# Loading q and k of a fused attention kernel by half batches into rings, and writing the result over the gate's tile

## The chip, the core and the metric

The kernel runs on one core of a Trainium2 chip. The time is the device time of one execution, in microseconds (us), as the median of several executions. Beside that there is one profiled execution, whose trace gives the start and the length of every instruction on each engine: TensorE (PE in the profile), VectorE (DVE), ScalarE (ACT), GpSimd (POOL, which does next to nothing here) and SyncE (SP), which issues the DMA transfers.

## What is computed

Attention within chunks of 64 tokens, on 8 batches of 8 heads, 576 tokens and 64 values per head, in float32; its heads side by side are the input x of a channel mix with 512 columns in and 1024 inside. Cut to what matters:

```python
# _attn_ref: q, k, v of [8, 8, 576, 64], chunks of 64 tokens
scores = scale * np.matmul(q_c, k_c.transpose(0, 1, 2, 4, 3))
scores = scores - np.max(scores, axis=-1, keepdims=True)
attn = np.exp(scores)
attn = attn / (np.sum(attn, axis=-1, keepdims=True) + 1e-09)
out = np.matmul(attn, v_c)
# _moe_ref: x of [8, 576, 512]
x_prev = np.concatenate([np.zeros((B, 1, D)), x[:, :-1, :]], axis=1)
xk = mu_k * x + (1.0 - mu_k) * x_prev
xr = mu_r * x + (1.0 - mu_r) * x_prev
k = np.maximum(xk @ w_k, 0.0)
v = k * k @ w_v
r = 1.0 / (1.0 + np.exp(-(xr @ w_r)))
return r * v
```

## The kernel before

The 8 x 576 tokens are one row of 4608, cut into 18 groups of 256 tokens (two tiles of 128). Since 576 is no multiple of 256, groups 2, 4, 6, 11, 13 and 15 lie across two batches; all but group 2, which the start loads in another layout, are loaded by `load_blocks`. Products that need more than one pass are done with operands split into a high and a low part (`xkhi`, `xklo`, `xrhi`, `xrlo`).

Two programs, written as strings of words, set the order of every instruction on every engine: nothing is moved by a scheduler. `START` sets up the weights and does groups 0 and 1 and the attention of group 2. `GROUP` is one period; `group(g)` emits it for g = 2 to 17 (this text calls it period g). Period g does the channel mix of group g, the attention of group g + 1, and the loads for groups after it. A word names a task and the steps of it that are emitted there:

- `Sc` are the scores of group g + 1 (64 matmuls in line 988, the first thing on PE in each period), the maximum, the exp and the sums behind them; `Pq` turns the normed p (line 1044) and multiplies it with v into `xps` (line 1062), from which x comes.
- `K0` to `K3` are the product with w_k (line 613), the relu and the square; `R0`, `R1` that with w_r (line 666) and the sigmoid, whose result is the gate's tile `sg` (five of them in turn).
- `V0`, `V1` (`moe_v`, periods 2 and 3, g < `SPLIT` = 4) are the product with w_v as it is (line 697), and `B`, `C` prepare pieces of w_v in these two periods; from period 4 on `H`, `Z` and `W` (`moe_halves`, line 887) do it with fewer products and more sums. The last step of either multiplies with the gate into a tile `out` (line 711 or 932), which is stored.
- `Lq`, `Lk` load q and k of group g + 3 (line 201), `Lv` the two v tiles of group g + 2 (line 180). `Dq.0` and `Dq.1` turn q and k of group g + 2 on DVE, whole tiles of 128 x 1024 in place (line 969). `Mk`, `Mr`, `Md` mix x with its predecessor.

All loads and stores are issued on SP, in the order of the words. One load of q or k for a group is 16 transfers, each for 32 of the 128 partitions and one of four pairs of heads, of 8 blocks of 32 tokens; where the group lies across two batches (`segments`) each of them is issued twice, so that there are 32:

```python
for s, n in segments(g * G, G):
    b, t0 = divmod(g * G + s, S)
    for j in range(2):
        for dh in range(2):
            for hp in range(HP):
                nc.sync.dma_start(out=dst[pp : pp + 32, hp, s // 32 : (s + n) // 32, :], in_=...)
```

The tiles for q and k are two each (pool `ld`), so the load for group g + 3 takes the tile whose group g + 1 has just had its scores. Groups 3 and 4 (`bq3`, `bk3`, `bq4`, `bk4`) are loaded in `START`, where v of tiles 6 and 7 (`v6`, `v7`) is loaded too.

Of the kernel before, what the change touches and what calls it, by code (L numbers as in the profile page):

```python
# [7 lines left out]
F32 = mybir.dt.float32  # L8
# [8 lines left out]
P = 128  # L17
CH = 64
# [63 lines left out]
def tile_chunk_attention_channel_mix(  # L82
# [13 lines left out]
    B, H, S, D = q.shape  # L96
# [6 lines left out]
    NG = B * S // G  # L103
# [5 lines left out]
    ld = ctx.enter_context(tc.tile_pool(name="ld", bufs=2))  # L109
# [46 lines left out]

    def load_nat(g):
        for nm, src in (("q", q), ("k", k)):
            do.task = f"n{nm}{g}"

            def fn(_, nm=nm, src=src):
                dst = T[f"{nm}{g}"] = ld.tile([P, H, 2, D], F32, tag=nm, name=f"{nm}n_{g}")
# [26 lines left out]
    def load_blocks(g):  # L189
        for nm, src in (("q", q), ("k", k)):  # L190
            do.task = f"b{nm}{g}"

            def fn(_, nm=nm, src=src):
                dst = T[f"{nm}{g}"] = ld.tile([P, HP, G // 32, 32], F32, tag=nm, name=f"{nm}_{g}")
                for s, n in segments(g * G, G):
                    b, t0 = divmod(g * G + s, S)
                    for j in range(2):
                        for dh in range(2):
                            pp = j * 64 + dh * 32
                            for hp in range(HP):  # L200
                                nc.sync.dma_start(  # L201
                                    out=dst[pp : pp + 32, hp, s // 32 : (s + n) // 32, :],
                                    in_=src[
                                        b, j * HP + hp, t0 : t0 + n, dh * 32 : (dh + 1) * 32
# [153 lines left out]

    def att_qk(t):

        g, tl = divmod(t, 2)
        tb = slice(tl * (TT // 32), (tl + 1) * (TT // 32))
        do.task = f"D{t}"
        for nm in "qk":

            def f_move(_, nm=nm):
                x = T[f"{nm}{g}"][:, :, tb, :]
                nc.vector.transpose(out=x, in_=x)

            do(f_move, "D")  # L370
# [314 lines left out]
    def moe_v(g, tls):  # L685
# [118 lines left out]
    def moe_halves(g):  # L804
# [122 lines left out]
        def scale(t, c, src):  # L927
            def fn(_):
                if f"o{g}{t}" not in T:
                    T[f"o{g}{t}"] = mo.tile([P, DM], F32, tag="out", name=f"out_{g}_{t}")  # L930
# [346 lines left out]
```

## Time and profile before

| | |
|---|---|
| median of 3 executions | 610.05 us (609.01 to 610.32) |
| the profiled execution | 606.43 us |
| its span in the trace | 604.5 us |
| granted TensorE clock, mean | 0.994 |
| busy PE, DVE, ACT | 98%, 76%, 59% of the span |

The span runs from the first to the last instruction of the trace, and the execution's own time is 1.93 us longer. Busy shares are means over the whole span; the place where an engine bounds the time is found in the chain of waits, which follows the work that ended last back to what released it, and in the timeline of an engine, which lists its instructions in order with the idle time in front of each and who ended it. For SP a row is a run of DMA issues, from the first issue to the last.

### The profile page before, as it was taken

The page shows a single profiled execution, that of the slowest core. Times are in us where ns is not written, and L with a number is a line of the kernel's source. Part 1 is how long each engine was busy: PE and PEld are TensorE (multiplying, and loading weights), DVE is VectorE, ACT ScalarE, POOL GpSimd, SP SyncE. Part 2 cuts the span into 40 slices and gives each one's busy share as a digit, 9 for nine tenths or more (in the row PEclk, how much of TensorE's full clock was granted, in tenths as well). Part 3 has the DMA queues.
Part 4 walks back from the last instruction along what each step waited for, and adds up shares of the span by engine and source line. Part 5 has one row for each costly group of instructions (what it writes and reads, how often), then busy time and mean ns, then how long its engine had stood idle before and what let it go on. Part 6 is the DMA issues. An engine that isn't in the chain of part 4 may idle for free.

```text
span 604.5 us, 15523 instructions
## 1 busy us (share of the span) xinstructions
PE 590.9 (98%) x6497; PEld 556.3 (92%) x6497; DVE 458.8 (76%) x743; ACT 355.1 (59%) x530; POOL 0.7 (0%) x6
## 2 busy tenths in 40 slices
PE   8899999999999999999999999999999999999997
PEld 7779999989997999999999999999997999999997
DVE  2799887659788687878787878887887488876734
ACT  4898963625647383838383838383828174646461
POOL 0000000000000000000000000000000000000000
PEclk9999999999999999999999999999999899999999
DMA  9995323244124344343122441243323343010000
GB/s 283 232 315 133 89 51 76 36 96 102 30 34 96 72 96 101 61 97 68 54 35 41 103 103 31 34 101 68 79 35 86 62 107 71 36 37 36 1 36 36
DMA packets 187573, 49.28 MB, mean 82 GB/s; under 512 B 173160, under 2 KB 179312, under 8 KB 187504
## 3 DMA queue, kind: packets, MB, share of 16 engines
q1 hardware_dynamic: 187488, 48.29, 35.6%
q8 instruction: 51, 0.84, 0.6%
q14 instruction: 18, 0.15, 0.1%
q10 hardware_dynamic: 16, 0.00, 0.0%
HBM read 38.80 MB, written 9.44 MB: 80 GB/s over the span
## 4 chain that ended last, share of the span: by engine, by line
PE 79%; SPq 13%; DVE 3%; DMA 2%; issue 2%; ACT 1%; DVEq 0%
PE pk L613 29%; PE pr L666 14%; PE vx L887 11%; SPq L201 10%; PE vyz L887 8%; PE pv L697 6%; SPq L180 3%; PE xps L1062 2%; PE s L988 2%; PE pt L1044 1%; DMA v<-in_v 1%; PE trq L345 1%; PE trk L345 1%; DMA qn<-in_q 1%; PE mxk L557 1%
## 5 line engine op out<-in xcount | busy, mean ns | idle before, releaser
L613 PE MATMUL pk<-xkhi,wk 128*128 128x256 f32 x1152 | 210.1, 283 | 0.0
L613 PEld LDWEIGHTS pk<-xkhi,wk 128*128 128x128 f32 x1152 | 178.2, 188 | 1.2
L613 PE MATMUL pk<-xklo,wk 128*128 128x256 f32 x576 | 162.3, 282 | 0.0
L633 ACT ACTIVATE rr<-pk 128x512 f32<-128x512 f32 x56 | 33.2, 592 | 128.7 <-PE pk L613 128.7
L613 PEld LDWEIGHTS pk<-xklo,wk 128*128 128x128 f32 x576 | 108.6, 189 | 0.1
L666 PE MATMUL pr<-wr,xrhi 128*128 128x512 f32 x288 | 95.2, 412 | 0.0
L887 PE MATMUL vx<-b,ks 128*128 128x256 f32 x504 | 66.7, 282 | 0.0
L666 PEld LDWEIGHTS pr<-wr,xrhi 128*128 128x128 f32 x288 | 52.7, 192 | 11.0
L887 PEld LDWEIGHTS vx<-b,ks 128*128 128x128 f32 x504 | 62.8, 189 | 0.0
L666 PE MATMUL pr<-wr,xrlo 128*128 128x512 f32 x144 | 57.8, 401 | 0.0
L697 PE MATMUL pv<-b,kk 128*128 128x256 f32 x384 | 46.7, 282 | 0.0
L697 PEld LDWEIGHTS pv<-b,kk 128*128 128x128 f32 x384 | 46.1, 188 | 0.3
L887 PE MATMUL vyz<-b,kk 128*128 128x256 f32 x336 | 44.5, 282 | 0.0
L887 PEld LDWEIGHTS vyz<-b,kk 128*128 128x128 f32 x336 | 41.9, 189 | 0.0
L724 DVE TENSOR_TENSOR kk<-rr,kk 128x1024 fp32r<-128x1024 f32 x28 | 33.1, 1222 | 9.3 <-ACT kk L871 9.1
L724 DVE TENSOR_TENSOR xklo<-mk,xkhi 128x1024 fp32r<-128x1024 f32 x15 | 18.4, 1225 | 24.5 <-ACT xkhi L1134 24.5
L916 ACT ACTIVATE u<-vx 128x256 f32<-128x256 f32 x28 | 10.7, 384 | 44.0 <-PE vx L887 44.0
L640 ACT ACTIVATE rr<-rr 128x512 f32<-128x512 f32 x56 | 35.4, 632 | 1.8
L666 PEld LDWEIGHTS pr<-wr,xrlo 128*128 128x128 f32 x144 | 27.7, 192 | 6.6
L1017 DVE TENSOR_REDUCE z<-p 128x16 f32<-128x1024 f32 x15 | 18.3, 1220 | 18.3 <-ACT p L1013 18.3
L1124 DVE SCALAR_TENSOR_TENSOR mk<-d,mu,x 128x256 f32<-128x256 f32 (+3 forms) x80 | 27.7, 413 | 0.4
L1062 PEld LDWEIGHTS xps<-pT,v 64*64 64x64 f32 x960 | 17.5, 137 | 10.9 <-DMA v<-in_v 5.1
(138 smaller groups left out, 957.1 us busy)
## 6 DMA issues: line engine op xcount, KB each, us to landing
v<-in_v SPq DMA_DIRECT2D x144, 64.0 KB, 2.4
out<-out SPq DMA_DIRECT2D x36, 256.0 KB, 2.4
k<-in_k SPq DMA_DIRECT2D x160, 32.0 KB, 1.9
q<-in_q SPq DMA_DIRECT2D x160, 32.0 KB, 2.0
wk_st<-in_moe_w_k SPq DMA_DIRECT2D x4, 1024.0 KB, 11.2
wv_st<-in_moe_w_v SPq DMA_DIRECT2D x4, 1024.0 KB, 8.8
wr_st<-in_moe_w_r SPq DMA_DIRECT2D x2, 1024.0 KB, 7.6
q<-in_q SPq DMA_DIRECT2D x48, 24.0 KB, 1.8
```

Source lines behind the costliest of these rows:

```text
L180: nc.sync.dma_start(out=vt[j * CH : (j + 1) * CH, :, e, :], in_=v[b, j * HP : (j + 1) * HP, c * CH : (c + 1) * CH, :].rearrange("h t d -> ...
L201: nc.sync.dma_start(out=dst[pp : pp + 32, hp, s // 32 : (s + n) // 32, :], in_=src[b, j * HP + hp, t0 : t0 + n, dh * 32 : (dh + 1) * 32].r ...
L613: nc.tensor.matmul(pk[:, e, :], wk[a][:, cb, f * P : (f + 1) * P], xk[b][:, cb, :], start=(n == 0), stop=(n == 3 * NB - 1),)
L633: nc.scalar.activation(r, T[f"pk{g}{fp}"], AF.Relu)
L640: nc.scalar.activation(r, r, AF.Square)
L666: nc.tensor.matmul(pr, xr[a][:, cb, tl * TT : (tl + 1) * TT], wr[b][:, cb, :], start=(n == 0), stop=(n == 3 * NB - 1),)
L697: nc.tensor.matmul(T[f"pv{g}{tl}"][:, cols[c]], kk[a][:, f, tok[tl]], quarter(f // HF, c)[:, b, f % HF, :], start=(f == 0 and n == 0 and c ...
L724: nc.vector.tensor_tensor(to, x, y, ALU.subtract)
L887: nc.tensor.matmul(to, a[i][:, f, :], weight(w, j, f), start=first and f == 0 and n == 0, stop=f == HF - 1 and n == 2, skip_group_check=True,)
L1017: nc.vector.tensor_reduce(out=T[f"z{g}"], in_=p(), axis=AX.X, op=ALU.add)
L1062: nc.tensor.matmul(T[f"xps{g}"][halves[c], 2 * j + a, tl * TT + e * CH : tl * TT + (e + 1) * CH], T[f"v{2 * g + tl}"][halves[j], hp, e, :] ...
L1124: nc.vector.scalar_tensor_tensor(out=to[:, cb, s : s + w], in0=T[f"d{g}"][:, cb, s : s + w], scalar=mu[:, cb : cb + 1], in1=T[f"xg{g}"][:, ...
```

## The change

q and k get one tile each for the whole run, a ring of 18 blocks of 32 tokens (one batch of 576 tokens), in place of two tiles of 8 blocks. What is loaded at a time is a half batch m of 9 blocks, in 16 transfers for q and 16 for k; a half batch never lies across two batches. `START` loads the 12 blocks 24 to 35 in one go in place of groups 3 and 4 (32 transfers of 12 blocks; `bq4` and `bk4` are gone), and half batch m = 4 to 15 is loaded in the period that `load_period` gives, which is the first whose scores are the last readers of the slots: periods 2 to 7 and 9 to 14, none in period 8.

The turn of a group is cut in two: `De`, the blocks that lay there before this period, stands where `Dq.0` stood, for q and for k; `Dl`, the blocks that come with this period's load, stands late in the period, behind `B.3` in periods 2 and 3 and behind `W.11` from period 4 on. A turn whose blocks run over the ring's end is two instructions. There are late turns of 4, 3, 2, 1 blocks in periods 2 to 5 and of 6, 5, 4, 3, 2, 1 in periods 9 to 14. The score matmuls read their columns from the rings.

The result is no longer a tile of its own: the product with the gate is written over the gate's tile `sg`, and the store reads that.

```diff
@@ START
-hwv3.1:D bq4.0 S5.3:A V001.6 V001.7 P4.1:A S5.4:D K13.3:A S5.5:D P4.2 K11.1:A K13.4:D D7.1:D
+hwv3.1:D S5.3:A V001.6 V001.7 P4.1:A S5.4:D K13.3:A S5.5:D P4.2 K11.1:A K13.4:D D7.1:D
...
-V10.3 V11.2 V11.3 Mk5.0:D V10.4 Mk5.1:D Mr4.1:A V11.4 D7.0:D bk4.0 Mk4.2:A V10.5 v6.0 V10.6
+V10.3 V11.2 V11.3 Mk5.0:D V10.4 Mk5.1:D Mr4.1:A V11.4 D7.0:D Mk4.2:A V10.5 v6.0 V10.6
...
@@ GROUP
-Sc.0 K0.0 Lq Lk Sc.1 Sc.2 K0.12 Mr.0 Dq.0 Sc.3 K0.34 K1.0 K1.12 E.0 Mr.1 Sc.4567 Mr.2 K1.34 K2.0 K2.12 E.1 H.0 K2.34
-K3.0 Pq.0 K3.12 Dq.1 Z.0 Pq.1 K3.34 Z.1 H.1 H.3 Z.2 H.4 Z.3 H.2 H.5 Z.456
+Sc.0 K0.0 Lq Lk Sc.1 Sc.2 K0.12 Mr.0 De.01 Sc.3 K0.34 K1.0 K1.12 E.0 Mr.1 Sc.4567 Mr.2 K1.34 K2.0 K2.12 E.1 H.0 K2.34
+K3.0 Pq.0 K3.12 Z.0 Pq.1 K3.34 Z.1 H.1 H.3 Z.2 H.4 Z.3 H.2 H.5 Z.456
...
-V0 V1.0 W.0 W.1 W.2 W.5 W.6 W.7 Mk.1 C.0 C.2 C.4 W.8 B.2 Mk.2 B.3456 C.1 C.3 C.5 V1.12345678 W.9 W.10 W.12 W.11 W.3 W.4 W.13 W.14 W.15 W.16
+V0 V1.0 W.0 W.1 W.2 W.5 W.6 W.7 Mk.1 C.0 C.2 C.4 W.8 B.2 Mk.2 B.3 <Dl.01 B.456 C.1 C.3 C.5 V1.12345678 W.9 W.10 W.12 W.11 >Dl.01 W.3 W.4 W.13 W.14 W.15 W.16
...
-    ld = ctx.enter_context(tc.tile_pool(name="ld", bufs=2))
+    ld = ctx.enter_context(tc.tile_pool(name="ld", bufs=1))
...
+    NBLK = S // 32
+    HB = NBLK // 2
+    ring = {nm: ld.tile([P, HP, NBLK, 32], F32, name=f"{nm}_ring") for nm in "qk"}
+
+    def slots_of(first, many):
+
+        a = first % NBLK
+        n = min(many, NBLK - a)
+        return [(0, a, n)] + ([(n, 0, many - n)] if n < many else [])
...
-    def load_blocks(g):
+    def load_blocks(name, first, many):
+        b, s = divmod(first, NBLK)
+        assert s + many <= NBLK
...
-                dst = T[f"{nm}{g}"] = ld.tile([P, HP, G // 32, 32], F32, tag=nm, name=f"{nm}_{g}")
-                for s, n in segments(g * G, G):
-                    b, t0 = divmod(g * G + s, S)
+                for n0, a, n in slots_of(first, many):
+                    t0 = (s + n0) * 32
                     for j in range(2):
                         for dh in range(2):
                             pp = j * 64 + dh * 32
                             for hp in range(HP):
                                 nc.sync.dma_start(
-                                    out=dst[pp : pp + 32, hp, s // 32 : (s + n) // 32, :],
+                                    out=ring[nm][pp : pp + 32, hp, a : a + n, :],
...
+    def turn(nm, first, many):
+        for _, a, n in slots_of(first, many):
+            x = ring[nm][:, :, a : a + n, :]
+            nc.vector.transpose(out=x, in_=x)
...
-                o = mo.tile([P, DM], F32, tag="out", name=f"out_{g}_{tl}")
+                o = T[f"sg{g}{tl}"]
                 nc.vector.tensor_tensor(o, T[f"pv{g}{tl}"], T[f"sg{g}{tl}"], ALU.mult)
...
-                o = T[f"o{g}{t}"]
-                nc.vector.tensor_tensor(o[:, cols[c]], src(), T[f"sg{g}{t}"][:, cols[c]], ALU.mult)
+                o = T[f"sg{g}{t}"]
+                nc.vector.tensor_tensor(o[:, cols[c]], src(), o[:, cols[c]], ALU.mult)
...
     def group_scores(g):
-        do.task = f"D{g}q"
-        for nm in "qk":
-
-            def f_move(_, nm=nm):
-                nc.vector.transpose(out=T[f"{nm}{g}"], in_=T[f"{nm}{g}"])
-
-            do(f_move, "D")
+        b0, b1 = 8 * g, 8 * g + 8
+        m = (b1 - 1) // HB
+        late = max(b0, HB * m) if load_period(m) == g - 2 else b1
+        for part, (first, last) in enumerate(((b0, late), (late, b1))):
+            do.task = f"D{g}{'el'[part]}"
+            for nm in "qk":
+                if first < last:
+                    do(lambda _, nm=nm, first=first, last=last: turn(nm, first, last - first), "D")
+
+    def load_period(m):
+
+        return max(2, -(-(HB * m - 25) // 8))
...
-    load_blocks(3)
-    load_blocks(4)
+    load_blocks("3", 24, 12)
...
     def group(g):
-        if g + 3 < NG:
-            load_blocks(g + 3)
+        now = [m for m in range(4, 2 * B_) if load_period(m) == g]
+        for m in now:
+            load_blocks(f"m{m}", HB * m, HB)
...
         for word in GROUP.split():
+            if word[0] in "<>":
+                if (word[0] == "<") != (g < SPLIT):
+                    continue
+                word = word[1:]
```

SP, from the second half of the start to the loads of period 2, before. `in_q`, `in_k` and `in_v` are the arrays in memory, `q_...`, `k_...`, `v_...` the tiles; `32x4x32` is partitions x blocks x tokens of one transfer.

```order
L201 DMA q_1009<-in_q 32x8x32 x16
L180 DMA v_1032<-in_v 64x4x64 x4
L201 DMA q_1134<-in_q 32x4x32 x32
L180 DMA v_1221<-in_v 64x4x64 x4
L713 DMA out<-out_0_1233 128x512
L713 DMA out<-out_1_1268 128x512
L201 DMA k_1385<-in_k 32x4x32 x32
L180 DMA v_1427<-in_v 64x4x64 x4
L713 DMA out<-out_1_1473 128x512
L713 DMA out<-out_0_1477 128x512
L201 DMA q_1541<-in_q 32x8x32 x16
L201 DMA k_1558<-in_k 32x8x32 x16
```

The same place now:

```order
L218 DMA q_ring<-in_q 32x12x32 x16
L196 DMA v_1026<-in_v 64x4x64 x4
L196 DMA v_1182<-in_v 64x4x64 x4
L727 DMA out<-sg_0_625 128x512
L727 DMA out<-sg_1_628 128x512
L196 DMA v_1353<-in_v 64x4x64 x4
L218 DMA q_ring<-in_q 32x9x32 x2
L727 DMA out<-sg_1_906 128x512
L218 DMA q_ring<-in_q 32x9x32
L727 DMA out<-sg_0_884 128x512
L218 DMA q_ring<-in_q 32x9x32 x13
L218 DMA k_ring<-in_k 32x9x32 x16
```

The 32 + 32 transfers of 4 blocks are gone, three of the v loads follow each other with only stores between them, and period 2 loads 9 blocks where it loaded 8.

SP in period 3, before, where group 6 lies across two batches:

```order
L201 DMA q_1952<-in_q 32x6x32 x16
L201 DMA q_1952<-in_q 32x2x32 x16
L201 DMA k_1985<-in_k 32x6x32 x16
L201 DMA k_1985<-in_k 32x2x32 x16
L180 DMA v_2193<-in_v 64x4x64 x4
L180 DMA v_2198<-in_v 64x4x64 x4
L713 DMA out<-out_0_2290 128x512
L713 DMA out<-out_1_2359 128x512
```

and now:

```order
L218 DMA q_ring<-in_q 32x9x32 x16
L218 DMA k_ring<-in_k 32x9x32 x16
L196 DMA v_2081<-in_v 64x4x64 x4
L196 DMA v_2086<-in_v 64x4x64 x4
L727 DMA out<-sg_0_2091 128x512
L727 DMA out<-sg_1_2111 128x512
```

Each of q and k is 16 transfers of 9 blocks where it was 16 of 6 and 16 of 2.

DVE at the end of period 2 and the head of period 3, before. `bs` are the sums of pieces of w_v (`B`), `out` the result, `m` and `p` the maximum and the exponent of the next scores, `mr` the mixed x, `kk` the squares:

```order
L724 TENSOR_TENSOR bs_1771<-bs_1771 128x1024
L743 TENSOR_TENSOR bs_1772<-b_876 128x1024
L724 TENSOR_TENSOR bs_1771<-bs_1772,bs_1771 128x1024
L724 TENSOR_TENSOR bs_1772<-bs_1772,bs_1771 128x1024
L711 TENSOR_TENSOR out_1_1891<-pv_1_1835,sg_1_1769 128x512
L1004 TENSOR_REDUCE m_2018<-s_1894 128x16
L1010 TENSOR_TENSOR p_2020<-s_1894,m_2018 128x2x8x64
L1124 SCALAR_TENSOR_TENSOR mr_2027<-d_1774,mu_100,x_1753 128x256 x4
L969 STREAM_TRANSPOSE q_1541<-q_1541 128x1024
L649 TENSOR_TENSOR kk_3_2035<-relu_0_2022,kk_3_2034 128x512
```

and now:

```order
L738 TENSOR_TENSOR bs_1693<-bs_1693 128x1024
L379 STREAM_TRANSPOSE q_ring<-q_ring 128x4x128
L379 STREAM_TRANSPOSE k_ring<-k_ring 128x4x128
L757 TENSOR_TENSOR bs_1694<-b_871 128x1024
L738 TENSOR_TENSOR bs_1693<-bs_1694,bs_1693 128x1024
L738 TENSOR_TENSOR bs_1694<-bs_1694,bs_1693 128x1024
L725 TENSOR_TENSOR sg_1_1691<-pv_1_1756,sg_1_1691 128x512
L1024 TENSOR_REDUCE m_1906<-s_1816 128x16
L1030 TENSOR_TENSOR p_1908<-s_1816,m_1906 128x2x8x64
L1144 SCALAR_TENSOR_TENSOR mr_1915<-d_1696,mu_100,x_1675 128x256 x4
L379 STREAM_TRANSPOSE q_ring<-q_ring 128x4x160
L379 STREAM_TRANSPOSE k_ring<-k_ring 128x4x160
```

Two turns of 4 blocks stand between the sums of `B`, and at the head of period 3 q and k are turned together, 5 blocks (4 x 160 columns) each.

DVE at the end of period 9, before; `u` are the sums of `moe_halves`, `vx` and `vyz` its products:

```order
L923 TENSOR_TENSOR u_9_4837<-u_9_4837,vx_4822 128x256
L932 TENSOR_TENSOR out_1_4904<-u_9_4837,sg_1_4811 128x256
L923 TENSOR_TENSOR u_9_4836<-u_9_4836,vyz_4823 128x256
L932 TENSOR_TENSOR out_0_4907<-u_9_4836,sg_0_4793 128x256
L923 TENSOR_TENSOR u_9_4836<-u_9_4836,vyz_4823 128x256
L932 TENSOR_TENSOR out_1_4904<-u_9_4836,sg_1_4811 128x256
L932 TENSOR_TENSOR out_0_4907<-vx_4822,sg_0_4793 128x256
L1004 TENSOR_REDUCE m_5050<-s_4926 128x16
L1010 TENSOR_TENSOR p_5052<-s_4926,m_5050 128x2x8x64
```

and now:

```order
L937 TENSOR_TENSOR u_9_4643<-u_9_4643,vx_4628 128x256
L944 TENSOR_TENSOR sg_1_4617<-u_9_4643,sg_1_4617 128x256
L379 STREAM_TRANSPOSE q_ring<-q_ring 128x4x192
L379 STREAM_TRANSPOSE k_ring<-k_ring 128x4x192
L937 TENSOR_TENSOR u_9_4642<-u_9_4642,vyz_4629 128x256
L944 TENSOR_TENSOR sg_0_4599<-u_9_4642,sg_0_4599 128x256
L937 TENSOR_TENSOR u_9_4642<-u_9_4642,vyz_4629 128x256
L944 TENSOR_TENSOR sg_1_4617<-u_9_4642,sg_1_4617 128x256
L944 TENSOR_TENSOR sg_0_4599<-vx_4628,sg_0_4599 128x256
L1024 TENSOR_REDUCE m_4822<-s_4732 128x16
```

Two turns of 6 blocks stand in front of the last sums, and the product with the gate goes into `sg`.

## Rows read from the trace of the kernel before

**Rows 1.** The page: busy shares, and DMA issues (KB each, us to landing).
```profile
PE 590.9 (98%) x6497; PEld 556.3 (92%) x6497; DVE 458.8 (76%) x743; ACT 355.1 (59%) x530; POOL 0.7 (0%) x6
...
q<-in_q SPq DMA_DIRECT2D x160, 32.0 KB, 2.0
```

**Rows 2.** The chain of waits in order of time: start us, us, engine, line.
```profile
138.75 1.09 PE s L988 x64
...
170.57 1.09 PE s L988 x64
...
203.22 1.09 PE s L988 x64
...
233.61 1.09 PE s L988 x64
...
311.84 2.99 PE pr L666 x12
...
324.79 1.09 PE s L988 x64
...
385.58 1.09 PE s L988 x64
...
467.19 5.34 PE pr L666 x12
...
482.51 1.09 PE s L988 x64
```

**Rows 3.** PE's timeline at the head of period 2: start us, us, line.
```profile
104.94 1.16 PE L988 MATMUL s<-k,q 64*64 64x64 f32 x64
```

**Rows 4.** The waits: engine, line, waited for, us in total, times, longest.
```profile
PE xps L1062 <- DMA v<-in_v: 3.5, 10, 0.5
```

**Rows 5.** SP's timeline, start and periods 2 and 12: start us, us, line, count.
```profile
102.68 16.15 SPq L201 DMA_DIRECT2D k<-in_k  x32
118.92 2.58 SPq L180 DMA_DIRECT2D v<-in_v  x4
...
122.72 8.27 SPq L201 DMA_DIRECT2D q<-in_q  x16
...
425.13 16.63 SPq L201 DMA_DIRECT2D q<-in_q  x32
441.81 17.28 SPq L201 DMA_DIRECT2D k<-in_k  x32
459.18 5.25 SPq L180 DMA_DIRECT2D v<-in_v  x8
```

**Rows 6.** SP's timeline at the head of period 7, before its loads.
```profile
264.32 0.84 SPq L935 DMA_DIRECT2D out<-out  x2
```

**Rows 7.** Two stretches: PE, PEld, DVE, ACT, POOL busy, granted clock, DMA, GB/s.
```profile
462.50:465.50 3.00, 1.85 (x41) 1.16 (x40) 2.90 (x4) 2.89 (x5) 0.00 (x0) 1.00 0.43 98
465.50:472.30 6.80, 6.50 (x36) 5.13 (x37) 6.07 (x11) 2.43 (x3) 0.00 (x0) 0.50 0.55 133
```

**Rows 8.** Groups of instructions by shape: busy us, mean ns of one.
```profile
L969 DVE STREAM_TRANSPOSE k<-k 128x1024 f32<-128x1024 f32 x14 | 17.4, 1240 | 5.0 <-DMA k<-in_k 4.9
...
L368 DVE STREAM_TRANSPOSE k<-k 128x512 f32<-128x512 f32 x2 | 1.4, 708 | 0.0
```

**Rows 9.** The waits again, for the sums behind the exp.
```profile
DVE z L1017 <- ACT p L1013: 18.3, 13, 2.7
```

**Rows 10.** DVE's timeline at the end of period 8.
```profile
322.51 0.42 DVE L932 TENSOR_TENSOR out<-u,sg 128x256 f32<-128x256 f32 x1
```

**Rows 11.** DVE and PE, end of period 2 and head of period 3.
```profile
133.09 0.69 DVE L711 TENSOR_TENSOR out<-pv,sg 128x512 f32<-128x512 f32 x1 [4.67 <-PE pv L697]
...
147.10 0.69 DVE L649 TENSOR_TENSOR kk<-relu,kk 128x512 fp32r<-128x512 f32 x1 [0.54 <-ACT kk L135]
...
149.45 1.23 DVE L1027 TENSOR_TENSOR p<-p,z 128x1024 f32<-128x1024 f32 x1
...
151.26 1.04 PE L1044 MATMUL pt<-ident,p 128*128 128x128 f32 x8
```

More of the change, by code (lines that the diff above doesn't have):

```diff
@@ L95, in tile_chunk_attention_channel_mix @@
     nc = tc.nc
-    B, H, S, D = q.shape
+    B_, H, S, D = q.shape
     DM, FF = w_k.shape
@@ L102, in tile_chunk_attention_channel_mix @@
     NCH = S // CH
-    NG = B * S // G
+    NG = B_ * S // G
     out_f = out.rearrange("b s c -> (b s) c")
@@ L155, in segments, with rows @@
         return [(0, many)]
+    NBLK = S // 32
[5 more added lines that the diff above has]
+        return [(0, a, n)] + ([(n, 0, many - n)] if n < many else [])
+    def rows(nm):
+        return ring[nm].rearrange("p h t i -> p h (t i)")
     def load_nat(g):
@@ L161, in fn @@
             def fn(_, nm=nm, src=src):
-                dst = T[f"{nm}{g}"] = ld.tile([P, H, 2, D], F32, tag=nm, name=f"{nm}n_{g}")
+                at = g % 2 * 2 * H * D
+                dst = T[f"{nm}{g}"] = ring[nm].rearrange("p h t i -> p (h t i)")[
+                    :, at : at + 2 * H * D
+                ].rearrange("p (h r d) -> p h r d", h=H, r=2)
                 for s, n in segments(g * G, G):
@@ L357, in move_qk @@
                 do(f_move, "A")
+    def turn(nm, first, many):
+        for _, a, n in slots_of(first, many):
+            x = ring[nm][:, :, a : a + n, :]
+            nc.vector.transpose(out=x, in_=x)
     def att_qk(t):
-        g, tl = divmod(t, 2)
-        tb = slice(tl * (TT // 32), (tl + 1) * (TT // 32))
         do.task = f"D{t}"
         for nm in "qk":
-            def f_move(_, nm=nm):
-                x = T[f"{nm}{g}"][:, :, tb, :]
-                nc.vector.transpose(out=x, in_=x)
-            do(f_move, "D")
+            do(lambda _, nm=nm: turn(nm, 4 * t, 4), "D")
     def att_scores(t):
@@ L928, in fn @@
             def fn(_):
-                if f"o{g}{t}" not in T:
-                    T[f"o{g}{t}"] = mo.tile([P, DM], F32, tag="out", name=f"out_{g}_{t}")
-                o = T[f"o{g}{t}"]
-                nc.vector.tensor_tensor(o[:, cols[c]], src(), T[f"sg{g}{t}"][:, cols[c]], ALU.mult)
+                o = T[f"sg{g}{t}"]
+                nc.vector.tensor_tensor(o[:, cols[c]], src(), o[:, cols[c]], ALU.mult)
                 if T.setdefault(f"done{g}{t}", 0):
@@ L981, in f_s @@
             T[f"s{g}"] = ps_s.tile([P, 2, 2, HP, CH], F32, tag="s", name=f"s_{g}")
-            qT, kT = (T[f"{nm}{g}"].rearrange("p h t i -> p h (t i)") for nm in "qk")
             for tl in range(2):
@@ L985, in f_s @@
                     for e in range(2):
[L986 removed]
+                        ((_, a, n),) = slots_of(8 * g + 4 * tl + 2 * e, 2)
                         for j in range(2):
@@ L989, in f_s @@
                                 T[f"s{g}"][halves[e], j, tl, hp, :],
-                                qT[halves[j], hp, col],
-                                kT[halves[j], hp, col],
+                                rows("q")[halves[j], hp, a * 32 : (a + n) * 32],
+                                rows("k")[halves[j], hp, a * 32 : (a + n) * 32],
                                 start=True,
@@ L1224, in group @@
         names_of = {
-            "Lq": [f"bq{g + 3}"],
-            "Lk": [f"bk{g + 3}"],
+            "Lq": [f"bqm{m}" for m in now],
+            "Lk": [f"bkm{m}" for m in now],
             "Lv": [f"v{2 * g + 4}", f"v{2 * g + 5}"],
-            "Dq": [f"D{g + 2}q"],
+            "De": [f"D{g + 2}e"],
+            "Dl": [f"D{g + 2}l"],
             "Sc": [f"S{g + 1}c"],
```

7 lines of the change are left out of this document (2 added, 5 removed).

## The prediction, made before the changed kernel had run

> **What bounds the kernel now.** First the page's busy shares: TensorE (PE) is busy 98% of the span [rows 1], so a change can only give back PE's gaps or slow its stream. Second the chain of waits in order of time, of which I read one thing, where the score matmuls of each group (line 988) start, since they open every period of `group(g)` [rows 2]. From group 4 on a period without a wait lasts 30.39 us (203.22 to 233.61); groups 2 and 3, which do moe_v whole, take 31.82 (138.75 to 170.57). Against these, three stretches are too long. Period 2 (its scores start at 104.94 [rows 3]) lasts 33.8 to 138.75, less 0.1 as the two views mark a start differently: 1.9 over. Period 4 lasts 32.65: 2.26 over. From 385.58 to 482.51 lie three periods, 96.93 for 91.17: 5.76 over. Together 9.9 us.
>
> Third, what PE waits for there: the attention's second product xps waits for v's load, ten times [rows 4], in period 2, in period 4 and shortly before 467. Fourth, why v is late, in SP's own rows [rows 5]. SP issues all loads and stores in one queue. Before the v of 118.92 stand 32 transfers of k that took 16.15 us; before the v of 459.18 stand 64 transfers of q and k, 33.9 us, more than a period, and v is issued the moment they are through. Such a double load comes wherever a group lies across two batches (groups 4, 6, 11, 13, 15): each half transfer is issued twice. With v (5.25) and two stores (0.84 [rows 6]) SP then needs 40 us for a period of 30.39, and the lag passes on.
>
> Fifth, the clock. In the 3.0 us from 462.5 PE was busy 1.85; the granted clock then stood at 0.50, the 1.2 GHz level, from 465.5 to 472.3 [rows 7], and the twelve matmuls of line 666 took 5.34 us [rows 2] for 2.99 elsewhere. So 2.35 of the 5.76 is clock, 3.4 is waiting. The page TensorE: Matmul & The Clock Gate of the Trainium skill (What's actually happening) says that one kernel shows slow matmuls in numbers that differ from run to run; this trace shows one stretch in one execution, and no number below needs the sentence.
>
> **The change, part by part.**
>
> *Loads.* Half batches never cross a batch, so every load is 16 + 16 transfers, and after the start 640 small transfers become 416 (before, 15 groups of 32 and 5 double ones of 32 more; now 12 blocks and 12 half batches of 32 each). What a transfer costs SP hardly depends on its size: 16.15/32 = 0.50 us with 4 blocks of 32 tokens, 8.27/16 = 0.52 with 8, 33.9/64 = 0.53 with 6 and 2 mixed [rows 5]. For 9 blocks, which no row shows, the ends are 0.52 (no growth) and 0.58 (0.52 x 9/8, growth with bytes); I take 0.55, nearer to the flat rows: 32 x 0.55 = 17.6 us. With v and the stores SP needs 17.6 + 5.25 + 0.84 = 23.7 us of 30.39 in every period, so it never lags. bk4 and bq4 leave START; v of tiles 6 and 7 then follows q's load directly, and the v that was issued at 118.92 comes some 16 us sooner, against a wait of 2. All three stretches end: -9.9 us, and nothing else of the loads is on PE's path. On the same path a wait could appear behind a first transfer that waits for the scores that free its slots; but SP reaches it only after the stores of the group before, at 264.32 + 0.84 [rows 6], when the scores that started at 264.0 (233.61 + 30.39 [rows 2]) and took 1.09 are over.
>
> *Early turns.* De now holds q and k together where before k's turn came later. A turn of 1024 columns takes 1.24, one of 512 0.71 [rows 8], so 0.18 plus 1.04 per 1024. At most 1.24 is moved ahead of the sums z; VectorE (DVE) idles there 18.3 us over 13 periods for ACT's exp [rows 9], 1.4 in the mean. Cost nothing; without that cover the normed p would come 1.2 later against PE's transpose.
>
> *Late turns.* In ten periods the last blocks arrive in the same period and are turned at its end, q and k. Data: SP starts the load 1.2 after the scores start (265.16 against 264.0 [rows 2, 6]), 17.6 for the issue and 2.0 for landing as for the 8-block ones [rows 1]: 20.8. The turn's place, behind W.11, begins 1.86 before the next scores (322.51 + 0.42 against 324.79 [rows 2, 10]), at 28.5. So 7.7 us of cover. What stands behind it on DVE are W.3, W.4 and the last scalings, which end a group and whose stores SP waits for; PE waits for the turn alone, with the next scores. Longest is period 9, 6 blocks, 0.18 + 0.78 = 0.96 each, 1.9 for both: it ends as the scores begin, and the first blocks there were turned early. I take 0.1 for it and nothing for the smaller ones.
>
> *Period 2 to 3.* This one costs. From V0's product at 133.09 to the turn of q in period 3 DVE works without a gap of any size [rows 11]. Two turns of 4 blocks go in: 1.4. In period 3 De turns 5 blocks of each, 1.65, for 1.24: another 0.4. The gap of 0.54 ahead of kk takes some; the shift is 1.3 at the normed p. That ended at 149.45 + 1.23 = 150.68, and PE's transpose began at 151.26: 0.58 of slack. So 0.7 us there, and I add 0.1, an estimate from no row, for kk and pT that come late with it. Ends: 0 (DVE regains it) and 1.8 (neither gap nor slack is real). I take 0.8. The scores of period 3 need the late turn only in their second half, and it ends about as they start. Period 3 has the same with 3 blocks, but longer gaps on DVE ahead of the exp's sums; nothing there.
>
> *Result over the gate's tile.* The product runs in place on the same shapes; the tile is held until its store has landed, a few us into the next period, and its next writer, a sigmoid, comes 14 us or more later. The wait for an older `out` goes. Nothing.
>
> *PE's scores* get up to 17 more waits in a period on semaphores that are long up; period 3's scores carry such waits already in the old program and take 1.09 as everywhere [rows 2]. Nothing.
>
> Sum, on the profiled execution's own time: 606.43 - 9.9 + 0.9 = 597.4.
>
> That execution is 3.62 us under the median of the runs, 610.05. The offset is unknown in kind: it goes with the stalls (further lag, a second stretch at 1.2 GHz behind one of the other two waits, 2.35), or it is fixed. Ends: 597.4 and 601.0. I let one stretch of 2.35 go and 1.27 stay: **598.7 us**.
>
> **The rivals.**
>
> *The clock stretch is not the stall's.* Then it falls elsewhere in the same number: 598.7 + 2.35 = 601.0. For it: the waits in periods 2 and 4 brought none in this trace, whose clock is at full level there. Against it: it begins where PE had been busy for only 1.85 of 3.0 us [rows 7].
>
> *The lag is not what makes v late* (v waits for its tile, which is freed by the xps before). Then nothing changes but 0.9 is added: 610 to 611, no change that can be measured. Against it: v at 459.18 starts 0.1 after k's last transfer (441.81 + 17.28), 30 us after the older xps.
>
> *SP pays by the block, and the late turn becomes the bound (slower).* The place is the turn at 28.5. If a transfer of 9 blocks cost x, data is there at 3.2 + 32x; from x = 0.79 on the turn is late, and at 0.83 ten periods 1.1 late each eat the gain of 11.4. Priced from the 4-block row by the block, 0.126 x 9 = 1.13, the data comes at 39.4, 10.9 late, and ten such periods give 598.7 + 109 = 708 us. Against it: 4 blocks and 8 cost the same within 3%. The page DMA: Bandwidth & Descriptors of the Trainium skill (Bandwidth, Measured) calls transfers under 64 KB descriptor-dominated, and since the change keeps the descriptors and only makes fewer transfers of them, by that rule the queue would gain nothing; for SP's issue time the rows here disagree with it.
>
> *The offset is fixed and period 3 costs double:* 601.0 + 0.9 = 601.9.
>
> **How the numbers follow.** Forecast 0.60 (598.7), clock stretch elsewhere 0.17 (601.0), fixed offset 0.14 (601.9), v late for another reason 0.06 (610), by the block 0.03. The range takes the first three with their ends: 596.5 would be no cost at all and the whole offset gone, less 0.7 for the spread of the runs, 595.8; above, 601.9 plus one clock stretch, 604.2. A difference of 0.2%, 1.2 us, is about what a measurement can tell from none. Faster 0.91, same 0.06, slower 0.03.
>
> **What would show it.** Right: no wait of xps for v; from period 4 on every period 30.39; 32 transfers for each load in 17 to 18 us; no stretch at 1.2 GHz after the start; period 3 at 32 to 33. Wrong: scores that wait for DVE's turn at a period's head, turns that wait for k's load, SP rows of 0.7 us or more a transfer, or waits at xps that stay.

## The result, and the profile after

The changed kernel takes 601.32 us in the median (601.20 to 601.41 in four executions), the kernel before 609.01 us (607.0 to 610.32 in five); the ratio is 0.9872, with a 95% interval of 0.9847 to 0.9898. A fifth execution of the changed kernel took 3104.1 us at a clock of 1.000; it is left out of these numbers, and nothing here tells what it waited for. The kernel is faster by 7.7 us, 1.3% of its time, and the time lies in the range. The profiled execution took 601.20 us, 5.2 us less than that of the kernel before; the forecast for this number was 597.4. So what went was more than 5.2, and something came in its place that the forecast had priced at nothing.

SP's timeline in period 5 (start us, us, line, count; answers to [rows 5, 6]):

```profile
200.44 0.84 SPq L947 DMA_DIRECT2D out<-sg  x2
201.38 8.35 SPq L218 DMA_DIRECT2D q_ring<-in_q  x16
209.77 8.62 SPq L218 DMA_DIRECT2D k_ring<-in_k  x16
218.49 5.96 SPq L196 DMA_DIRECT2D v<-in_v  x8
```

The queue is done 24.6 us after the scores began (199.89) and then has nothing to do until the next stores at 231.39. The 32 transfers of 9 blocks took 17.0 us here, 0.53 each; over the periods 3 to 14 a load takes from 16.8 to 18.5 us, 17.6 in the mean, which is 0.55 each. No wait of xps for v is left in the table of waits.

The two stretches of [rows 7], read from the trace of the changed kernel (us, then PE, PEld, DVE, ACT, POOL busy, granted clock, DMA, GB/s):

```profile
462.50:465.50 3.00, 3.00 (x62) 2.53 (x55) 2.27 (x2) 2.97 (x5) 0.00 (x0) 1.00 0.44 73
465.50:472.30 6.80, 6.80 (x56) 6.67 (x55) 5.23 (x11) 3.52 (x7) 0.00 (x0) 1.00 0.35 78
```

PE has no gap there, and the clock stays at its full level. What has come in its place stands in the chain of waits, at the score matmuls that open each period (start us, us, engine, line; answers to [rows 2]; the line is now 1008):

```profile
104.95 1.09 PE s L1008 x64
...
136.78 1.55 PE s L1008 x62
...
169.14 1.44 PE s L1008 x62
...
199.89 1.70 PE s L1008 x64
...
230.97 1.58 PE s L1008 x63
...
261.85 1.09 PE s L1008 x64
...
292.25 1.09 PE s L1008 x64
...
322.64 1.09 PE s L1008 x64
...
353.03 1.60 PE s L1008 x63
...
384.03 1.33 PE s L1008 x64
...
414.67 1.47 PE s L1008 x62
...
445.43 1.47 PE s L1008 x62
...
476.28 1.59 PE s L1008 x63
...
507.27 1.55 PE s L1008 x63
...
538.21 1.09 PE s L1008 x64
```

Two things are to be seen. The starts give the periods: periods 7, 8 and 9 last 30.4 us, as every period from 4 on should; periods 3 to 6 and 10 to 15 are 0.25 to 0.69 us too long. And in just those ten periods, the ones behind a late turn, the scores take 1.33 to 1.70 us in place of 1.09. Over the whole span it is one line of the groups by shape (busy us, mean ns of one):

```profile
L1008 PE MATMUL s<-k_ring,q_ring 64*64 64x64 f32 x960 | 21.8, 225 | 0.0
```

The same work is 17.4 us in the kernel before and 17.5 in a kernel shown below; by the chain, the ten periods' scores are together 4.4 us over 1.09 each. So 4.4 us of the gain went into the scores. The account of the two profiled executions, all from starts of scores: from the scores of period 2 to the last K0, the kernel before had 10.0 us above its undisturbed periods, 2.35 of them through the stretch at 1.2 GHz; the changed kernel has 4.9 us above them, 4.4 in the scores and some 0.5 in products further on. 10.0 - 4.9 = 5.1, and the trace ends 5.1 us sooner.

The end of period 2 and the head of period 3, on DVE and PE (answers to [rows 11]):

```profile
148.34 1.23 DVE L1047 TENSOR_TENSOR p<-p,z 128x1024 f32<-128x1024 f32 x1
...
149.75 1.04 PE L1064 MATMUL pt<-ident,p 128*128 128x128 f32 x8
```

The normed p ends 12.8 us after the period's start, before it was 11.9: 0.9 us later, for 1.3 priced. PE comes to its transpose right then, since its scores took 0.46 longer.

### The profile page after: what moved, and what is told of

Same layout as the page of the kernel before. It is cut to its first block, busy times and chain, and to the rows that moved or that the text cites. A ratio compares the mean times of both kernels' runs of the same rounds, so it can differ in the third digit from the quotient of the medians.

```text
span 599.4 us, 15446 instructions
## 1 busy us (share of the span) xinstructions
PE 589.2 (98%) x6497; PEld 556.8 (93%) x6497; DVE 459.2 (77%) x763; ACT 354.7 (59%) x530; POOL 0.7 (0%) x6
## 4 chain that ended last, share of the span: by engine, by line
PE 96%; DVE 2%; DMA 1%; ACT 0%; issue 0%; DVEq 0%
PE pk L627 35%; PE pr L680 17%; PE vx L901 13%; PE vyz L901 10%; PE pv L711 8%; PE s L1008 3%; PE xps L1082 3%; PE pt L1064 2%; PE trq L362 1%; PE trk L362 1%; DMA q_ring<-in_q 1%; PE mxk L571 1%; PE s L403 1%; PE mxr L571 1%; PE warm L1211 1%; PE pt L465 0%
## 5 line engine op out<-in xcount | busy, mean ns | idle before, releaser
L680 PE MATMUL pr<-wr,xrhi 128*128 128x512 f32 x288 | 93.3, 405 | 0.0
L847 DVE TENSOR_TENSOR ss<-rr 128x512 f32<-128x512 f32 x14 | 9.7, 692 | 28.2 <-ACT rr L654 28.2
L1144 DVE SCALAR_TENSOR_TENSOR mr<-d,mu,x 128x256 f32<-128x256 f32 (+3 forms) x80 | 27.5, 411 | 0.0
## 6 DMA issues: line engine op xcount, KB each, us to landing
wk_st<-in_moe_w_k SPq DMA_DIRECT2D x4, 1024.0 KB, 11.9
```

The costliest lines, as they stand in the source:

```text
L680: nc.tensor.matmul(pr, xr[a][:, cb, tl * TT : (tl + 1) * TT], wr[b][:, cb, :], start=(n == 0), stop=(n == 3 * NB - 1),)
L1144: nc.vector.scalar_tensor_tensor(out=to[:, cb, s : s + w], in0=T[f"d{g}"][:, cb, s : s + w], scalar=mu[:, cb : cb + 1], in1=T[f"xg{g}"][:, ...
```

## The experiments

Theory: the second pieces of the loads that lie across two batches make SP late, v with it, and the changed kernel loses 4.4 us because its scores have to wait for more semaphores than they can at no cost. (A semaphore is a counter: here a load or an engine raises it, and an instruction of another engine waits for it.) Rivals: v is late for its tile's sake; the scores are slow because data or the turn come late, or because of what is written into the ring beside them.

**e1_one_piece: the kernel before without the second pieces.**

```diff
-                for s, n in segments(g * G, G):
+                for s, n in [(0, G)]:
                     b, t0 = divmod(g * G + s, S)
+                    t0 = min(t0, S - G)
```

> The kernel before, but the groups that lie across two batches (4, 6, 11, 13, 15) are loaded in one piece, all 8 blocks from the end of the first of the two batches, so that every load of q or k is 16 transfers; these five groups are computed with other tokens than they should be, and nothing else differs. If the second pieces cause the stalls: no wait of xps for v, no stretch at 1.2 GHz, the three long stretches gone, 606.4 - 9.9 = 596.5 us in the profiled execution, and a median within 1 us of it, if the spread of the runs goes with the stalls too. If v is late for another reason (its own tile comes free late): 609 us as before. If the stretch at 1.2 GHz is not the stall's: about 599, with such a stretch somewhere.

Measured: 598.65 us in the median (596.73 to 598.98), ratio 0.9869 (0.983 to 0.9909) to the kernel before, which had 607.09 on this chip; the profiled execution took 596.73, for 596.5 expected. The median was expected within 1 us of that and lies 2 above it: the clock over the span reads 0.997 in the five other executions and 1.000 in the profiled one. The chain of waits in it, at the scores (line 989 here):

```profile
105.19 1.09 PE s L989 x64
...
137.01 1.09 PE s L989 x64
...
168.83 1.09 PE s L989 x64
...
199.22 1.09 PE s L989 x64
```

Periods 2 and 3 last 31.82 each, period 4 30.39, and so on to the end, and the clock falls nowhere in this trace: the whole of the 10 us, the stretch at 1.2 GHz included, hangs on the second pieces. v is late because of the queue. The first rival falls.

**e2_over_gate: the kernel before with the result over the gate's tile, and nothing else.**

```diff
-                o = mo.tile([P, DM], F32, tag="out", name=f"out_{g}_{tl}")
+                o = T[f"sg{g}{tl}"]
...
-                nc.vector.tensor_tensor(o[:, cols[c]], src(), T[f"sg{g}{t}"][:, cols[c]], ALU.mult)
+                nc.vector.tensor_tensor(o[:, cols[c]], src(), o[:, cols[c]], ALU.mult)
```

> The kernel before with one part of the change alone: the result is written over the gate's tile. Expected: no change, within 0.2% of the kernel before (609 us, 607 to 610.3). If the wait for an older result tile had been part of the stalls: up to 2 us faster. If holding the gate's tile until its store has landed delays a sigmoid: slower, with ACT waiting for DMA ahead of sg.

Measured: 608.28 us (603.48 to 612.42), ratio 1.0027 (0.9996 to 1.0059): no gain, and at most 0.6% lost. The table of waits has a row that the kernel before has not and the changed kernel has not either: ACT, ahead of the sigmoid, waits for a store of `sg` three times, 3.2 us in all and up to 2.0. The three stand in periods 4, 11 and 13, where the double loads hold up the stores on SP, and the chain of waits does not pass through them. The trace is of use for another question too. It has the waits for v too, and two falls of the clock behind them (columns as above):

```profile
122.50:125.80 3.30, 2.03 (x30) 1.17 (x32) 2.89 (x4) 1.78 (x2) 0.00 (x0) 1.00 0.67 188
125.80:129.20 3.40, 3.40 (x59) 2.90 (x51) 0.96 (x1) 1.03 (x1) 0.00 (x0) 0.50 0.42 94
467.20:470.60 3.40, 2.13 (x55) 1.51 (x55) 3.30 (x5) 1.45 (x3) 0.00 (x0) 0.99 0.68 210
470.60:474.00 3.40, 3.40 (x9) 2.63 (x9) 2.27 (x5) 2.80 (x3) 0.00 (x0) 0.50 0.36 59
```

PE was busy for 2.03 of 3.30 us and for 2.13 of 3.40, waiting for v, and then ran at the 1.2 GHz level. The first of these places, in period 2, had the same wait in the kernel before (1.99 of 3.00 us busy from 121.0) and no fall behind it; that period lasts 31.8 us undisturbed, 33.7 there and 35.6 here, so the fall costs as much again as the wait. Which of the waits has a fall behind it is not the same in the two traces.

**e3_touch: small matmuls that wait ahead of the scores.**

```diff
+            x = rows("k")[halves[1], hp, a * 32 : (a + 2) * 32]
+            nc.tensor.matmul(T[f"s{g}"][halves[0], 1, 0, hp, :], x, x, start=True, stop=True)
...
-... B.3 <Dl.01 B.456 C.1 C.3 C.5 V1.12345678 W.9 W.10 W.12 W.11 >Dl.01 ...
+... B.3 <Xl.0123 <Dl.01 B.456 C.1 C.3 C.5 V1.12345678 >Xl.01 W.9 W.10 >Xl.23 W.12 W.11 >Dl.01 ...
```

> The changed kernel, and in each of the ten periods with a late turn four additional matmuls of 64 x 64 on the raw k blocks just loaded, two ahead of W.9 and two ahead of W.12 (in periods 2 and 3 all four behind Mk.2 in the order of the words, ahead of the late turn); their result is overwritten by the scores. They wait for the loads' eight semaphores, so that the scores wait for DVE's turn alone. If the 4.4 us by which the scores are longer in these ten periods come from wait instructions in a stream of very short matmuls: the scores fall from 1.3 to 1.7 us back to 1.1, the new matmuls cost at most 0.05 us each among matmuls ten times as long, and the time is 596.5 to 599 us. If the scores are slow because data or the turn come late, or because DMA and DVE write into the ring beside them: 601.3 us or more.

Measured: 607.88 us, ratio 1.001 (0.9984 to 1.0036): the whole gain gone. PE's timeline at the end of period 5 tells why (line 1001 is the new matmul; each of the two in a row is two passes):

```profile
229.64 0.28 PE L901 MATMUL vyz<-b_q,kk 128*128 128x256 f32 x1
229.85 0.44 PE L1001 MATMUL s<-k_ring 64*64 64x64 f32 x4
230.22 1.70 PE L901 MATMUL vx<-b,ks 128*128 128x256 f32 x12
231.85 0.44 PE L1001 MATMUL s<-k_ring 64*64 64x64 f32 x4
232.22 1.69 PE L901 MATMUL vyz<-b,kk 128*128 128x256 f32 x12
233.75 1.58 PE L901 MATMUL vx<-b,ks 128*128 128x256 f32 x12
235.26 0.93 PE L1025 MATMUL s<-k_ring,q_ring 64*64 64x64 f32 x48
```

The scores are down to 1.09 again (943 ns from the first start to the last, in all ten periods), as the theory wants. But the matmuls start every 0.12 us in the products, and from the last one ahead of a pair (229.64) to the first one behind it (230.22) it is 0.58: a pair costs 0.46, and the 12 products behind it take another 0.11 longer (1.70 for 1.58). Such a period lasts 31.5, for 30.4: 0.28 us for each new matmul, where I had 0.05. The waits are not this price: each pair has two separate wait instructions, and they are done 2 us ahead of it (those of the pair at 229.85 start at 227.64 and 227.88). The price of a 64 x 64 matmul alone among others of 128 x 128 was not in the trace I started from. The Trainium skill says of it, in TensorEngine Tiling (Array Packing), Key Properties, that a change of the tiling mode drains TensorE. The rows fit that; how much of the 0.58 is the drain they don't tell.

**e4_late_first: the scores of the late blocks first.**

```diff
-            for tl in range(2):
+            comes = load_period((8 * g + 7) // HB) == g - 2
+            for tl in (1, 0) if comes else (0, 1):
```

> The changed kernel, but in the ten periods with a late turn the scores take the second tile of the group, which holds the late blocks, first. Work and waits are the same in number. If wait instructions in a stream of short matmuls are the cost: at the head of the scores PE's sequencer can do them while the last products of the period before still run, and most of 0.3 to 0.6 us is gone in the eight periods with at most 4 late blocks; 598 to 599.5 us. If the late turn itself is what the scores wait for: they now meet it up to 0.5 us sooner, and the time goes up, to 602 to 605 us.

Measured: 601.39 us (599.62 to 601.70), for 598 to 599.5 expected; the changed kernel itself was not timed beside it on this chip, and the profiled execution of e4 had a stretch at 1.2 GHz in the start, so the time decides nothing. The chain of waits tells more:

```profile
170.71 1.24 PE s L1009 x64
...
201.26 1.21 PE s L1009 x64
...
231.78 1.21 PE s L1009 x64
...
353.48 1.72 PE s L1009 x63
```

With the same waits in the same number, the scores of periods 4 to 6 fall from between 1.44 and 1.70 to about 1.2, 0.12 to 0.15 above the undisturbed, and those of 14 and 15 as far. There about half of the wait instructions are done ahead of the first score, while the products of the period before still run; the other four stand in the stream, in the open. Periods 12 and 13 fall less (1.27 and 1.32 for 1.47). Periods 3, 10 (353.48) and 11 stay long (1.48, 1.72 and 1.40): there the turn of k ends 0.3 us or less ahead of the scores, and no wait that stands behind it in the order can be done sooner. So late data are not the cost in the others. That half of the excess remains (2.3 of 4.4 us) leaves the question open until e6.

**e5_after_again, and e6_dh_outer: the same transfers in another order.**

> The changed kernel once more, unaltered, to stand beside the three others on the same chip. In the call before, the kernels had a stretch at 1.2 GHz of 3.4 us at 22 to 24 us, in the start, in most executions (the clock over the span then reads 0.997), which the first executions of the changed kernel did not show (0.999). Expected: 601.3 us without it, up to 603 us with it.

Measured: 603.22 us (601.38 to 603.63), ratio 0.9929 (0.9902 to 0.9955) to 607.56. Five of the six executions read a clock of 0.996 or 0.997 over the span, as the traces with the stretch in the start do (e2 apart, whose clock falls three times); the sixth, at 0.999, took 601.38, and its trace has no stretch.

```diff
-                    for j in range(2):
-                        for dh in range(2):
+                    for dh in range(2):
+                        for j in range(2):
                             pp = j * 64 + dh * 32
```

> The changed kernel, but the 16 transfers of a load are issued in another order: the half of the head's values outside, the half of the heads inside it. The eight DMA semaphores go round in the order of issue, so that the two transfers that one matmul's rows come from now use the same semaphore, and a score matmul waits for one in place of two; no separate wait instruction is needed on PE for the second one. Same transfers, same number, same turns. If the separate wait instructions are what lengthens the scores: in the ten periods with a late turn they fall from 1.3 to 1.7 us to 1.1 to 1.2 (period 10 may keep a part, its turn ends as the scores begin), and the time falls by 3.5 to 4.5 us against the changed kernel on the same chip. If waiting as such, or data that come late, is the cost: no change.

Measured: 599.03 us (597.15 to 599.25), 4.2 less than the changed kernel on the same chip. The programs differ on PE in this (the waits of the scores of period 5, from the first late block on; each of these is two matmuls of the trace). The changed kernel:

```
MATMUL s_2674<-k_ring,q_ring 64x64 [waits DMAHW4_49,DMAHW0_49,DVE_49]
MATMUL s_2674<-k_ring,q_ring 64x64 [waits DMAHW4_49,DMAHW0_49]
MATMUL s_2674<-k_ring,q_ring 64x64 x2
MATMUL s_2674<-k_ring,q_ring 64x64 [waits DMAHW5_49,DMAHW1_49] x2
```

and with the loops exchanged:

```
MATMUL s_2674<-k_ring,q_ring 64x64 [waits DMAHW4_49,DVE_49]
MATMUL s_2674<-k_ring,q_ring 64x64 [waits DMAHW0_49]
MATMUL s_2674<-k_ring,q_ring 64x64 x2
MATMUL s_2674<-k_ring,q_ring 64x64 [waits DMAHW5_49]
```

In the traces no weight load carries more than one wait; the others stand in semaphore instructions of their own ahead of it on PE, with one or two waits each. The trace of the changed kernel has eight of these, of 51 ns, at the scores of each of the ten periods (nine in the first of them), and none in periods 7 to 9; in periods 10 and 11 one and three of the eight are done ahead of the first score, in the others all stand among the scores. With the loops exchanged there is one (two in the first), and as many weight loads that wait as before. In the list of instructions of the line (ns shortest, median, longest), the changed kernel and then this one, with three and one of period 2 among them:

```profile
L1008 PEldq EVENT_SEMAPHORE  x84: 51/51/99, 102.7 to 508.4; - x84
...
L1008 PEldq EVENT_SEMAPHORE  x12: 51/51/211, 104.8 to 506.0; - x12
```

The scores, by shape and in period 5:

```profile
L1008 PE MATMUL s<-k_ring,q_ring 64*64 64x64 f32 x960 | 17.5, 221 | 0.0
```

```profile
201.63 1.16 PE L1008 MATMUL s<-k_ring,q_ring 64*64 64x64 f32 x64
```

17.5 us in place of 21.8, 1.16 in this view in place of 1.77. The cost was not the waiting but the separate wait instruction, in a stream where a matmul starts every 15 ns. In the changed kernel's trace one such instruction starts 0.125 us after the one before, for the most part, whether two or six matmuls stand between them, so that they set the pace. It takes a row of them: with the loops exchanged the one or two that are left stand among the scores in eight of the ten periods, and there the scores take 943 or 944 ns from the first start to the last, as in the kernel before. The Trainium skill has the mechanism in Perfetto Trace Analysis, Identifying Dependency Chains: an instruction that waits for several engines may have semaphore instructions put ahead of it. The trace agrees, for several semaphores of the loads. The price here: 0.24 to 0.61 us for eight of them where the matmuls are short, 0.12 to 0.15 with half of them ahead of the stream (e4, periods 4 to 6).

**e7_dh_outer_early: and the late turn sooner on DVE.**

```diff
-... W.8 B.2 Mk.2 B.3 <Dl.01 ... W.12 W.11 >Dl.01 W.3 ...
+... W.8 B.2 >Dl.01 Mk.2 B.3 <Dl.01 ... W.12 W.11 W.3 ...
```

> As the run before, and from period 4 on the late turn stands two places sooner on DVE, ahead of xklo, where DVE waits 1.3 us for ACT in every period. If only the wait instructions counted: the same time as the run before, and in period 10, where the turn of 6 blocks ended as the scores began, up to 0.5 us less. If DVE cannot hide the turns there: xklo and the first sums come later, and it is slower by up to 0.5 us in the periods with 5 and 6 blocks.

Measured: 598.77 us (596.93 to 599.26); without the stretch in the start 596.93 and 597.01, where e6 had 597.15. No difference that can be told: behind the exchange of the loops the place of the turn costs nothing, and 0.04 us of period 10 is all it had (its scores take 1.13 in e6 and 1.09 here).

**e8_q_twice: 48 transfers in place of 32.**

```diff
+                if nm == "q" and many == HB:
+                    ((_, a, _),) = pieces
+                    pieces = [(0, a, 5), (5, a + 5, 4)]
```

> The changed kernel with each half-batch transfer of q issued as two, of 5 and 4 blocks: 48 transfers a period in place of 32. At 0.52 us each they take 25 us; the data for the late turn come at 1.2 + 25 + 2 = 28.2 us into the period, just before the turn's place at 28.5, and SP needs 25 + 5.3 + 0.9 = 31.2 us for a period of 30.4, so that it falls behind by about 1 us in each of periods 3 to 7 and 9 to 14. If SP's issue time is the cover as priced: turns and then scores wait for the loads by about 1 us a period more and more, and the time is 606 to 615 us. If it is the transfers' bytes or the memory that set the landing: no change, 601 us.

Measured: 609.52 us, in a single execution. From the table of waits (in total, times, longest) and SP's timeline in period 9:

```profile
DVE k_ring L383 <- DMA k_ring<-in_k: 14.7, 7, 3.7
...
PEld s L1012 <- DVE k_ring L383: 5.9, 6, 2.5
```

```profile
325.54 16.43 SPq L222 DMA_DIRECT2D q_ring<-in_q  x32
342.02 8.72 SPq L222 DMA_DIRECT2D k_ring<-in_k  x16
350.84 6.08 SPq L196 DMA_DIRECT2D v<-in_v  x8
```

The 32 transfers of 4 and 5 blocks take 0.51 us each, 16 of 9 blocks 0.55: SP pays nearly by the transfer, and the same bytes in twice the transfers take 16.4 us where the changed kernel's q takes 9.2 in this period. With 16 more of them the turn waits for k and the scores for the turn. So the late turn does become the bound, as in the slower rival, but by the number of transfers and not by their blocks, and at the place that the prediction gave: with 32 transfers the load of period 9 is issued 19.8 us after the scores began and, with 2.0 for landing, has 6.7 us to spare before the turn's place at 28.5 (7.7 were said); with 48 it has 0.1.

**e9_turn_before_v0 and e10_e7_again: the turn of periods 2 and 3 in an idle stretch of DVE.**

```diff
-... Mk.2 B.3 <Dl.01 B.456 ...
+... Mk.2 B.3 B.456 ...
...
-V0 V1.0 W.0 ...
+V0.01234567 <Dl.01 V0.8 V1.0 W.0 ...
```

> As e7_dh_outer_early, and in periods 2 and 3 the late turn stands ahead of the first result's product (line 725), where DVE waits 3 to 5 us for PE, in place of between the sums of B. In e7 period 3 lasts 32.36 us for 31.82, and DVE works without a stop from that product over the two turns to the normed p. If the turns in that stretch are the cost, as the prediction had it for the boundary of periods 2 and 3: period 3 falls to 31.82, and the time by 0.5 us against e7 on the same chip. If the load lands too late for the sooner place, or the cost has another cause: no change, or slower by the wait.

> e7_dh_outer_early once more, to stand beside e9 on the same chip: 597.0 us in an execution without the stretch at 1.2 GHz in the start, 598.5 to 599.3 with it.

Measured: e9 597.15 us (596.38 to 598.21), ratio 0.9826 (0.9793 to 0.9859) to the 607.57 of before; e7 again 598.84 (596.69 to 599.27). The medians have different numbers of executions with a clock of 0.997 in them. At 1.000 three executions of e9 took 596.38 to 596.63 and the only one of e7 596.69, where 0.5 us of difference was expected; these times don't decide it. The chain does, of e7 (its first run) from period 2 to period 4, and then of e9 with period 3 between them:

```profile
104.94 1.09 PE s L1008 x64
...
169.12 1.09 PE s L1008 x64
```

```profile
105.02 1.09 PE s L1008 x64
...
136.84 1.09 PE s L1008 x64
...
168.66 1.09 PE s L1008 x64
...
199.05 1.09 PE s L1008 x64
```

The two periods last 64.18 us in e7 and 63.64 in e9. Period 2 lasts 31.82 in both, period 3 32.36 and 31.82. So the turns at that boundary did cost 0.54 us, and e9's trace has none of the costs left that the change brought in: its periods last 31.82 and 30.39 to the end. It is the fastest of the kernels here: the changed kernel, the two loops over a load's transfers exchanged, and the late turns at two other places.

## Why the prediction was right, and where it was not

*The stalls.* Right in cause and size: 9.9 us said, 10.0 gone, and e1 shows that the second pieces alone make them.

*The loads.* Right: 0.55 us for a transfer of 9 blocks in the mean of the loads, and 0.55 said. That the queue would gain nothing, because the descriptors stay the same, is not borne out: where a group lay across two batches, its load took 33.9 us and takes 17.6 now. e8 shows what sets the cover.

*The result over the gate's tile.* Nothing, as said, to within the 0.6% of e2. That no sigmoid would come soon enough to wait for the store held in the changed kernel; beside the double loads (e2) three of them did wait.

*Early and late turns from period 4 on.* 0.1 us was said, for the turn of 6 blocks in period 9. With the loops exchanged it is 0.04 (e6, the scores of period 10), and nothing in the other periods. In the changed kernel itself the turn and the wait instructions can't be told apart there: its 0.51 over is in the sum for the scores. (By the rows a turn takes 0.18 us and 1.06 for 1024 columns, not 1.04; for turns of 768 columns, which took 0.98 and 0.94 us, this changes nothing.)

*Period 2 to 3.* 0.8 said. In the changed kernel only 0.08 is to be seen beside the scores' 0.46, since PE was late by about as much as DVE; with the scores mended it comes out as 0.54 (e7), and goes with the turn's place (e9). The mechanism was right, the shift on DVE 0.9 in place of 1.3.

*PE's scores.* This is the step that failed: "up to 17 more waits in a period on semaphores that are long up; period 3's scores carry such waits already in the old program and take 1.09 as everywhere. Nothing." They cost 4.4 us. The row was right and the comparison wrong. The scores of the old period 3 have 16 weight loads that wait, most of them for one semaphore, and their four separate wait instructions are done 1.0 to 2.2 us before the first score starts, where PE's sequencer ran ahead of the array; in the changed kernel there are eight, and in eight of the ten periods all of them stand among the scores. The count of waits was no measure; how many an instruction has, and where it stands, is.

*The offset.* I took 3.62 us between the profiled execution and the median as stretches at 1.2 GHz and let 2.35 of it go. In the result all of it went: the changed kernel's profiled execution and its median are 0.12 apart. So there were two errors. The profiled execution took 3.8 us more than its sum (601.20 for 597.4), since 4.9 came in where 0.9 was priced, and 10.0 went for 9.9; and 1.15 us more of the offset went than was let go. They partly cancelled: 601.32 for 598.7. That is luck as much as working: in e5 the same kernel's median lies 1.84 above its profiled execution, at 603.22.

*The clock.* The forecast took the stretches for the stall's, and the rival had them elsewhere. With 23 executions of the kernel before on one chip there is more to say: they lie between 604.02 us, where the clock over the span is 1.000, and 611.69, where it is 0.986; e1, without the waits for v, stays at 0.997 or 1.000. So, as far as these clocks and the traces show, all stretches but one in the start go with the waits. Without any of them the gain is some 2.7 us: from the fastest execution of before, 604.0, to the changed kernel without a stretch, 601.2 to 601.4 on two other chips; and the account of the two traces without the 2.35 says the same (5.1 - 2.35 = 2.75). How much of the other 5 us of the median's 7.7 is clock is not shown: at one clock, 0.994, eight of the 23 executions lie between 604.43 and 610.71, so the waits themselves differ in length from execution to execution.

What is open: in five of the ten periods (5, 10, 13, 14 and 15) the products of line 901 run 1% slower (1.44 us for twelve matmuls in place of 1.42), about 0.5 us in all. With the loops exchanged that is gone too. It does not simply go with the number of wait instructions: e4 has as many, and the slower products in three of the five periods only. No run here tells the cause.

## What to carry to other kernels

Count an added wait by where it stands: a second semaphore on one instruction can be an instruction more on that engine, free where the engine's sequencer runs ahead, as at the head of a stream, and paid for where many of them follow each other among short matmuls. The order in which a load's transfers are issued decides how many semaphores its readers wait for, so transfers that one reader needs together should fall on the same one. And a short wait of TensorE may cost about as much again in clock (1.9 and 1.9 us in period 2 of e2), in some executions and not in others: look at the spread of the runs and their clocks before one profiled execution is taken for the time.

## What the runs showed of the hardware that was not expected

The issue of one transfer on SP took 0.50 us with 4 blocks of 32 tokens, 0.51 with 4 and 5 mixed and 0.55 in the mean with 9. A pair of 64 x 64 matmuls between products of 128 x 128 cost 0.57 us with what it adds to the products behind it, for 0.06 us in the stream of scores (four of its 64 passes, 943 ns in all). A separate wait instruction of 51 ns took 0.125 us of the stream of scores where eight followed each other, and nothing where one or two stood alone. And the start has a fall of the clock of its own in the traces of e2, e3, e4, e6 and the second run of e7, so with the change and without it: in e6 the windows read so (columns as above),

```profile
20.40:23.80 3.40, 1.56 (x57) 1.17 (x59) 1.84 (x3) 2.95 (x7) 0.00 (x0) 1.00 0.55 125
23.90:27.20 3.30, 3.30 (x68) 2.75 (x58) 0.00 (x0) 3.30 (x13) 0.00 (x0) 0.50 1.10 322
```

while in the profiled execution of e7, with 1.71 us busy in the first of these two stretches, the clock stayed at 1.00 in the second. It is worth some 2 us of 600: in e5 601.38 without it, and 602.92 to 603.63 in the executions at a clock of 0.996 or 0.997, whose traces were not kept.
